# Scores and their gradient computed as rows instead of columns in a one-core attention-and-MLP training step

## The chip, the cores and the metric

The kernel runs on one core of one Trainium2 chip. The metric is device time in microseconds of one execution; lower is better. The kernel before took 407.63 us (median of three runs, 407.42 to 408.31). The core has a matrix engine (TensorE; its matmuls are listed as PE and its weight loads as PEld), a vector engine (DVE), a scalar engine (ACT), GpSimd (POOL) and SyncE (SP, which here only issues DMAs). Each engine runs its own instructions strictly in order and waits on semaphores for the others.

## The reference, cut to what matters

The reference is the forward pass and all gradients of `g * A(x) + (1 - g) * B(x)` for one token. A is decode attention over a cache of 32 heads with 4096 keys of 128 elements in bf16; B is a small MLP with the mish activation; g is a sigmoid gate. What the change touches is, for each head,

```
s  = K @ q                       # 4096 scores
p  = softmax(s / sqrt(128))
o  = p @ V                       # forward output
dp = V @ do                      # do: gradient of o
ds = p * (dp - sum(p * dp))
dq = ds @ K / sqrt(128)
dK = ds (outer) q / sqrt(128)    # 4096 x 128, written out
dV = p (outer) do                # 4096 x 128, written out
```

K and V are read once (1 MB each per head) and dK and dV are written once (1 MB each per head), so a head moves 4 MB and all of the kernel some 164 MB.

## The kernel before, in words

The program is written with every engine's order fixed by hand: instructions are issued in the order of the Python text. One loop iteration handles one head `h`; `G = 4` heads form a group, whose weights (`wq`, `wo`) and whose MLP share are mixed into the iterations by the position `hh = h % 4` and a small hand-made budget.

A K tile is stored as 128 partitions x 32 rows (`J`) x 128 elements; partition p holds keys 32p to 32p + 31. To contract over the 128 elements, the head's tile is transposed first. `tr_block` (lines 510 to 515) views eight bf16 rows as four 128x128 blocks of 4-byte words, transposes the four on TensorE into one PSUM tile (`tr`, two buffers), and copies that with ACT into the SBUF tile `KT` or `VT`. Four such blocks make a head's K or V. A row of a block is two keys of 64 words each, so after the transpose partitions 0 to 63 belong to one key and 64 to 127 to the next, and the two halves of each word (even and odd elements) are two bf16 operands, the "parities".

`cols_mm` (lines 517 to 523) then makes the scores in the layout of the K tile, 128 partitions x 32 columns. For each of 16 pairs of columns and each parity, it loads 128 transposed columns as weights and streams 32 columns of `qz`, which hold q in two of them and zeros elsewhere, so each product adds into its own two columns of the same PSUM tile: 32 weight loads and 32 matmuls. `scores` does it for S (K and q), `dP` for DP (V and do). The wide zero-padded tiles `qz` and `doz` are filled by `pair_cp` (lines 233 to 237), once a group for each.

Iteration h issues, in this order for TensorE: `v_tr(h, 0)`, `dqo_mm(h - 1)`, `v_tr(h, 1)`, the maximum over all partitions (`softmax`, line 548), `v_tr(h, 2)`, `v_tr(h, 3)`, `dP(h)`, `k_tr(h + 1, 0)`, `k_tr(h + 1, 1)`, `zd_mm` (line 566, the sums for softmax), `k_tr(h + 1, 2)`, `k_tr(h + 1, 3)`, `scores(h + 1)`, `dq_o(h)`. The last (lines 605 to 614) makes dq and o as four-row products: the stationary operand has four columns, each of four products writes its own 32-partition quarter of one PSUM tile (`od4`), and 512 elements stream through each. `od_cp` copies that tile to SBUF, and `dqo_mm` (lines 620 to 624) brings it into columns with four fp32 products with a stationary operand of 128x128 and a 0/1 matrix of two columns.

The vector engine takes, per head: the maximum's negative `negM` (line 550), `dk_out(h - 1)` (two outer products of 1.2 us each, line 581), `pj` (line 562, needs DP), `rz`, `negD`, `p`, `ds` (lines 570 to 577), `dv_out(h)` (two outer products), the row maximum `m` of the next S (line 542), and then the group's extra work. ACT takes the transposes' copies, the exponential `exps`, `dgm` (line 544, needs `m`), `od_cp` and extras. SP issues the loads of K (four buffers) and V (three) and the stores of dK and dV (four buffers).

Of the kernel before, what the change touches and what calls it, by code (L numbers as in the profile page):

```python
# [7 lines left out]
ACT = mybir.ActivationFunctionType  # L8
ALU = mybir.AluOpType
# [7 lines left out]
def kernel(  # L17
# [25 lines left out]
    P = 128  # L43
# [139 lines left out]
    dx_parts = const.tile([P, RC, NG + 3], F32, name="dx_parts")  # L183

    p4b, ds4b = [], []
    qz = const.tile([P, G, 3 * J - 2], BF16, name="qz")
    doz = const.tile([P, G, 3 * J - 2], BF16, name="doz")
    nc.gpsimd.memset(qz[:], 0.0)
    nc.gpsimd.memset(doz[:], 0.0)
    for i in range(3):  # L190
        for lst, nm in ((p4b, "p4"), (ds4b, "ds4")):
            lst.append(const.tile([P, J * 4], BF16, name=f"{nm}{i}"))
# [38 lines left out]
        return ps  # L231

    def pair_cp(z, ps):
        for par in range(2):
            nc.vector.tensor_tensor(z[:, :, J - 2 + par * J:J + par * J],
                                    ps[:, par, :].unsqueeze(2).to_broadcast([P, G, 2]),
                                    half[:].unsqueeze(1).to_broadcast([P, G, 2]), ALU.mult)

    def g_qcol(g):
        groups[g]["col"] = col_mm(groups[g]["q_row"])  # L240
# [13 lines left out]
    def g_do(g, hh):  # L254
        gp = groups[g]
        junk = small.tile([P, D], BF16, name="junk", tag="junk", bufs=1)
        nc.vector.scalar_tensor_tensor(junk[:], in0=wos[g][:, hh, :], scalar=1.0, in1=da_bc[:],  # L257
                                       op0=ALU.mult, op1=ALU.mult, accum_out=gp["do_col"][:, hh:hh + 1])
# [251 lines left out]
    def tr_block(src, dst, c):  # L510
        tp = tr_ps.tile([P, TB // 2, P], F32, name="tr", tag="tr")
        words = src[:, c * TB:(c + 1) * TB, :].rearrange("p a b -> p (a b)").bitcast(F32)
        for t in range(TB // 2):
            nc.tensor.transpose(tp[:, t, :], words[:, t * P:(t + 1) * P], ident_f[:])  # L514
        nc.scalar.copy(dst[:, c * (TB // 2):(c + 1) * (TB // 2), :], tp[:])  # L515

    def cols_mm(out, T, z):
        Tb = T[:].rearrange("p c r -> p (c r)").bitcast(BF16).rearrange("p (c r a) -> p c r a", r=P, a=2)
        for c in range(J // 2):
            for par in range(2):  # L520
                a = J - 2 - 2 * c + par * J
                nc.tensor.matmul(out, lhsT=Tb[:, c, :, par], rhs=z[:, a:a + J],  # L522
                                 start=(c == 0 and par == 0), stop=(c == J // 2 - 1 and par == 1))

    def k_tr(h, c):
        if h < H:
            if c == 0:
                KT[h] = kvT.tile([P, J // 2, P], F32, name="KT", tag="KT")
            tr_block(kts[h], KT[h], c)

    def v_tr(h, c):
        if c == 0:
            VT[h] = kvT.tile([P, J // 2, P], F32, name="VT", tag="VT")
        tr_block(vts[h], VT[h], c)

    def scores(h):
        if h >= H:
            return
        S_ps[h] = s_ps.tile([P, J], F32, name="S", tag="S")
        cols_mm(S_ps[h][:], KT.pop(h), qz[:, h % G, :])  # L540
        m32 = small.tile([P, 1], F32, name="m32", tag="m32")
        nc.vector.reduce_max(m32[:], S_ps[h][:], axis=AX.X)  # L542
        dgms[h] = small.tile([P, P], F32, name="dgm", tag="dgm", bufs=1)
        nc.scalar.activation(dgms[h][:], ident_bf[:], ACT.Copy, scale=m32[:])  # L544

# [7 lines left out]
    def exps(h, negM):  # L553
        es[h] = small.tile([P, J], BF16, name="e_bf", tag="e_bf")
        zds[h] = small.tile([P, 2], F32, name="zd", tag="zd")
        nc.scalar.activation(es[h][:], S_ps.pop(h)[:], ACT.Exp, bias=negM[:], scale=scale, accum_out=zds[h][:, 0:1])

    def dP(h):
        DP_ps[h] = s_ps.tile([P, J], F32, name="DP", tag="DP")
        cols_mm(DP_ps[h][:], VT.pop(h), doz[:, h % G, :])  # L560
        pj = small.tile([P, J], F32, name="pj", tag="pj")
        nc.vector.scalar_tensor_tensor(pj[:], in0=DP_ps[h][:], scalar=1.0, in1=es[h][:],
                                       op0=ALU.mult, op1=ALU.mult, accum_out=zds[h][:, 1:2])

    def zd_mm(h, mx):
# [2 lines left out]
    def probs(h, mx):  # L568
        rz = small.tile([P, 1], F32, name="rz", tag="rz")
        nc.vector.reciprocal(rz[:], mx[:, P:P + 1])  # L570
        negD = small.tile([P, 1], F32, name="negD", tag="negD")
        nc.vector.tensor_scalar(negD[:], mx[:, P + 1:P + 2], rz[:], -1.0, ALU.mult, ALU.mult)
        p4s[h] = p4b[h % 3][:, 0:J * 4].rearrange("p (j t) -> p j t", t=4)
        nc.vector.tensor_scalar(p4s[h], es.pop(h)[:].unsqueeze(2).to_broadcast([P, J, 4]), rz[:], None, ALU.mult)
        ds4s[h] = ds4b[h % 3][:, 0:J * 4].rearrange("p (j t) -> p j t", t=4)
        nc.vector.scalar_tensor_tensor(ds4s[h], in0=DP_ps.pop(h)[:].unsqueeze(2).to_broadcast([P, J, 4]),  # L576
                                       scalar=negD[:], in1=p4s[h], op0=ALU.add, op1=ALU.mult)
        zds.pop(h)

# [13 lines left out]
    def dv_out(h):  # L593
        out_pair(h, dVv, p4s[h], groups[h // G]["do_row"])
# [106 lines left out]
    k_tr(0, 3)  # L701
    for hh in range(G):
        g_do(0, hh)
    scores(0)
    g_dodiag(0)
    g_dobc(0)
    g_docol(0)
    g_dopair(0)
# [2 lines left out]
    for h in range(H - 1):  # L711
        g, hh = h // G, h % G
        nx, pv = g + 1 < NG, g > 0
        v_tr(h, 0)
        if hh == 0 and pv:
            g_docol(g)
        if hh == 3 and nx:
            g_qcol(g + 1)
        if h > 0:
            dqo_mm(h - 1)  # L720
        v_tr(h, 1)
        mx, negM = softmax(h)
        if h > 0:
            dqo_red(h - 1)
        if hh == 0 and pv:
            g_dopair(g)
        if h > 0:
            dk_out(h - 1)
        v_tr(h, 2)
        v_tr(h, 3)  # L730
        exps(h, negM)
        dP(h)
        k_tr(h + 1, 0)
        k_tr(h + 1, 1)
        zd_mm(h, mx)
        if hh == 0 and pv:
            f_new(g - 1)
            f_diag(g - 1)
        if hh == 1 and pv:
            f_dx(g - 1, 3)  # L740
        if hh == 2 and nx:
            g_do(g + 1, 0)
        if hh == 3 and nx:
            g_qpair(g + 1)
            g_do(g + 1, 3)
        probs(h, mx)
        if hh == 3 and nx:
            g_qpair_cp(g + 1)
        k_tr(h + 1, 2)
        k_tr(h + 1, 3)  # L750
        if hh == 0 and pv:
            f_o4(g - 1)
            f_bc(g - 1)
        if hh == 3 and nx:
            g_dodiag(g + 1)
        dv_out(h)
        scores(h + 1)
        dq_o(h)
        od_cp(h)
        load_k(h + KBUFS)  # L760
        load_v(h + VBUFS)
        if h == H - 4:
            assert dw2_next[0] == FCN
            for a, b in W2P:
                nc.sync.dma_start(dw2_v[:, a:b, :], w2_sb[:, a:b, :])
            nc.sync.dma_start(out_8[FM:F, :], w2_sb[0:FT, FR, :])
        if h == H - 2:
            assert not mq
            nc.sync.dma_start(db1_row, dh_bc[0:1, :])
            nc.sync.dma_start(dw1_v[:, 0:3, :], w1_sb[:, 0:3, :])  # L770
            nc.sync.dma_start(dw1_v[:, 3:RC, :], w1_sb[:, 3:RC, :])
        budget = 0.0
        if hh == 0:
            if nx:
                g_new(g + 1)
            if pv:
                f_o4c(g - 1)
                f_aT_pe(g - 1)
                f_dx(g - 1, 0)
                f_dx(g - 1, 1)  # L780
                f_dx(g - 1, 2)
                f_aT_add(g - 1)
                f_dwo(g - 1, 0)
                f_dwo(g - 1, 1)
            budget = 0.9
        if hh == 1:
            if pv:
                f_dx(g - 1, 4)
                for c in range(RC):
                    f_dwq(g - 1, c)  # L790
                f_dwq_st(g - 1)
                f_dwo(g - 1, 2)
                f_dwo(g - 1, 3)
                f_dwo_st(g - 1)
            budget = 2.7
        if hh == 2:
            if nx:
                g_do(g + 1, 1)
                g_do(g + 1, 2)
                g_q(g + 1)  # L800
            budget = 0.9
        if hh == 3:
            if g % 2 == 0 and g + 2 < NG:
                load_wqp(g // 2 + 1)
            if g + 2 < NG:
                load_wo(g + 2)
            if nx:
                g_dobc(g + 1)
                g_qs(g + 1)
            budget = 2.7  # L810
        if h >= 2:
            mlp_some(budget)
            dw2_some(2)
# [15 lines left out]
    v_tr(h, 2)  # L829
    v_tr(h, 3)  # L830
    exps(h, negM)
    dP(h)
    zd_mm(h, mx)
    f_bc(g, 0, 3)
# [83 lines left out]
```

## Time and profile before

| | |
|---|---|
| median of three runs | 407.63 us |
| profiled execution, its own time | 409.23 us |
| its span in the profile | 407.4 us |
| granted TensorE clock, mean over the span | 0.89 |
| matmuls of S, DP (line 522) | 34.2 and 37.0 us busy, 1024 of each |
| weight loads for them | 32.3 and 34.0 us busy |
| transposes, K and V (line 514) | 78.6 and 90.2 us busy, 512 of each |
| ACT copies of the transposes (line 515) | 69.8 and 72.6 us, 128 of each, 588 and 585 ns each |
| DVE outer products (line 581) | 150.4 us, 128 |

The profile is one execution. Its page gives each engine's busy time, the span in 40 slices, DMA queues, a chain of work followed back from the last instruction, and groups of instructions by line. Further views of the same trace give the instructions in order of time (the timeline), what an engine waited for, and busy time, clock and DMA share by windows of time. A matmul's end is modelled, so gaps between a matmul and what it releases are read between starts where possible.

### The profile page before, as it was taken

To read this page: it belongs to the slowest core of one execution; us is meant where nothing else is said; L and a number is where in the kernel's file an instruction comes from. 1 tells how busy PE (TensorE), PEld (TensorE's weight loads), DVE (VectorE), ACT (ScalarE), POOL (GpSimd) and SP (SyncE) were. 2 spreads that over 40 slices of the span, in tenths; PEclk is the share of its full clock that TensorE was granted. 3 is DMA by queue.
4 is the path that set the end of the run, shared out by engine and by line. 5 is a ranking of instruction groups with operands and counts; after the bars stand their busy time and mean duration, and the time that the engine had idled before them with its cause. 6 is when DMAs were issued, how large, how long until landed. Compare 5 with 4: busy or idle time off the path is not lost.

```text
span 407.4 us, 10856 instructions
## 1 busy us (share of the span) xinstructions
PE 332.7 (82%) x4445; PEld 271.9 (67%) x4445; DVE 306.6 (75%) x845; ACT 232.6 (57%) x479; POOL 10.0 (2%) x25
## 2 busy tenths in 40 slices
PE   2698998889898998989898898879989798989600
PEld 1487776677686977877677678758777676877500
DVE  3646774797898587998999785666899987995640
ACT  2345556666476453765567666765776553776520
POOL 3000001000000000000000003000000000000000
PEclk9989999989898597999999896787999987899755
DMA  8999999999999999999999999999999999999883
GB/s 290 427 415 422 416 414 404 403 420 421 417 421 423 422 419 421 414 426 421 424 424 425 426 418 425 416 426 422 424 408 405 426 417 425 422 386 421 359 333 133
DMA packets 28695, 164.76 MB, mean 404 GB/s; under 512 B 2916, under 2 KB 3045, under 8 KB 12262
## 3 DMA queue, kind: packets, MB, share of 16 engines
q1 hardware_dynamic: 28338, 164.05, 97.8%
q8 instruction: 35, 0.57, 0.5%
q14 instruction: 14, 0.11, 0.1%
q0 software_dynamic: 256, 0.01, 0.0%
q10 hardware_dynamic: 52, 0.01, 0.0%
HBM read 82.03 MB, written 82.03 MB: 403 GB/s over the span
## 4 chain that ended last, share of the span: by engine, by line
DVE 44%; PE 34%; ACT 10%; issue 5%; DMA 2%; DVEq 0%; ACTq 0%; SPq 0%
DVE o_sb L581 22%; PE tr L514 15%; PE dqo_ps L624 7%; DVE junk L327 3%; PE DP L522 3%; ACT od_sb L618 2%; DVE junk L257 2%; DVE ds L576 2%; DMA wq_p<-in_A_wq_dram 2%; PE q_ps L210 2%; PE od L611 2%; PE mx L548 2%; ACT KT L515 2%; ACT VT L515 2%; ACT wo_g L385 2%
## 5 line engine op out<-in xcount | busy, mean ns | idle before, releaser
L515 ACT COPY VT<-tr 128x512 f32<-128x512 f32 x128 | 72.6, 585 | 43.3 <-PE tr L514 41.4
L514 PE MATMUL tr<-ident_f,Vn 128*128 128x128 f32 x512 | 90.2, 314 | 3.4 <-ACT VT L515 1.8
L515 ACT COPY KT<-tr 128x512 f32<-128x512 f32 x128 | 69.8, 588 | 39.4 <-PE tr L514 38.7
L514 PE MATMUL tr<-ident_f,Kn 128*128 128x128 f32 x512 | 78.6, 301 | 8.7 <-DMA Kn<-in_A_k_cache_dram 5.9
L514 PEld LDWEIGHTS tr<-ident_f,Vn 128*128 128x128 f32 x512 | 69.1, 166 | 15.0 <-ACT VT L515 7.3
L581 DVE TENSOR_TENSOR o_sb<-qs_row,ds 128x2048 bf16<-128x2048 bf16 x64 | 75.2, 1217 | 0.3 <-DMA out_dram<-o_sb 0.3
L581 DVE TENSOR_TENSOR o_sb<-do_row,p 128x2048 bf16<-128x2048 bf16 x64 | 75.2, 1217 | 0.0
L514 PEld LDWEIGHTS tr<-ident_f,Kn 128*128 128x128 f32 x512 | 61.3, 154 | 13.6 <-DVE ident_f L165 5.8
L544 ACT ACTIVATE dgm<-ident_bf,m 128x128 f32<-128x128 bf16 x32 | 12.8, 401 | 57.8 <-DVE m L542 48.6
L550 DVE TENSOR_REDUCE negM<-mx 128x1 f32<-128x128 f32 x32 | 9.3, 291 | 44.8 <-PE mx L548 34.0
L624 PE MATMUL dqo_ps<-sel,od_sb 128*128 128x2 f32 x256 | 37.2, 267 | 6.8 <-ACT od_sb L618 5.1
L624 PEld LDWEIGHTS dqo_ps<-sel,od_sb 128*128 128x128 f32 x256 | 35.5, 215 | 9.7 <-ACT od_sb L618 7.3
L522 PE MATMUL DP<-doz,VT 128*128 128x32 bf16 x1024 | 37.0, 180 | 2.3
L522 PEld LDWEIGHTS <-VT 128*128 128x128 bf16 x1024 | 34.0, 100 | 6.4 <-ACT VT L515 4.3
L522 PEld LDWEIGHTS <-KT 128*128 128x128 bf16 x1024 | 32.3, 97 | 6.0 <-ACT KT L515 3.2
L522 PE MATMUL S<-qz,KT 128*128 128x32 bf16 x1024 | 34.2, 177 | 1.9
L611 PE MATMUL od<-Kn,ds 128*4 128x512 bf16 x256 | 33.3, 382 | 0.0
L611 PE MATMUL od<-Vn,p 128*4 128x512 bf16 x256 | 33.3, 382 | 0.0
L257 DVE SCALAR_TENSOR_TENSOR junk<-wo_g,da_bc 128x640 bf16<-128x640 bf16 x32 | 26.3, 820 | 0.4
L385 ACT ACTIVATE wo_g<-da_bc,o 128x640 bf16<-128x640 bf16 x32 | 24.6, 820 | 0.0
L327 DVE SCALAR_TENSOR_TENSOR junk<-wq_p,dq_bc 128x512 bf16<-128x512 bf16 x35 | 24.0, 687 | 0.5
L618 ACT COPY od_sb<-od 128x512 f32<-128x512 f32 x32 | 18.2, 568 | 1.4 <-PE od L611 1.2
(171 smaller groups left out, 337.4 us busy)
## 6 DMA issues: line engine op xcount, KB each, us to landing
out_dram<-o_sb SPq DMA_DIRECT2D x64, 1024.0 KB, 15.1
Kn<-in_A_k_cache_dram SPq DMA_DIRECT2D x32, 1024.0 KB, 17.2
Vn<-in_A_v_cache_dram SPq DMA_DIRECT2D x32, 1024.0 KB, 17.9
wq_p<-in_A_wq_dram SPq DMA_DIRECT2D x4, 1280.0 KB, 14.7
wo_g<-in_A_wo_dram SPq DMA_DIRECT2D x8, 640.0 KB, 16.9
out_dram<-wo_g SPq DMA_DIRECT2D x8, 640.0 KB, 17.5
out_dram<-wq_p SPq DMA_DIRECT2D x4, 1280.0 KB, 16.3
w_sb<-in_B_w_dram SPq DMA_DIRECT2D x1, 2160.0 KB, 23.1
```

What stands on the lines that cost most here:

```text
L257: nc.vector.scalar_tensor_tensor(junk[:], in0=wos[g][:, hh, :], scalar=1.0, in1=da_bc[:], op0=ALU.mult, op1=ALU.mult, accum_out=gp["do_col ...
L327: nc.vector.scalar_tensor_tensor(junk[:, cs], in0=wqs[g][:, c, cs], scalar=1.0, in1=gp["dq_bc"][:, cs], op0=ALU.mult, op1=ALU.mult, accum_ ...
L385: nc.scalar.activation(wos[g][:, hh, :], da_bc[:], ACT.Copy, scale=groups[g]["o4"][:, hh:hh + 1])
L514: nc.tensor.transpose(tp[:, t, :], words[:, t * P:(t + 1) * P], ident_f[:])
L515: nc.scalar.copy(dst[:, c * (TB // 2):(c + 1) * (TB // 2), :], tp[:])
L522: nc.tensor.matmul(out, lhsT=Tb[:, c, :, par], rhs=z[:, a:a + J], start=(c == 0 and par == 0), stop=(c == J // 2 - 1 and par == 1))
L544: nc.scalar.activation(dgms[h][:], ident_bf[:], ACT.Copy, scale=m32[:])
L550: nc.vector.tensor_reduce(negM[:], mx[:, 0:P], axis=AX.X, op=ALU.max, negate=True)
L581: nc.vector.tensor_tensor(dst[:, a:b, :].rearrange("p j (k t) -> p j k t", t=4), row.rearrange("p (k t) -> p k t", t=4).unsqueeze(1).to_br ...
L611: nc.tensor.matmul(od4[32 * c:32 * c + 4, :], lhsT=c4[:, 4 * jb:4 * jb + 16].rearrange("p (j t) -> p t j", t=4)[:, 0, :], rhs=N[:, jb:jb + ...
L618: nc.scalar.copy(od_sb[h][:].rearrange("p j d -> p (j d)"), od4[:])
L624: nc.tensor.matmul(od_sb[h][:], lhsT=t[:, j, :], rhs=sel[:, :, j], start=(j == 0), stop=(j == 3))
```

## The change

Four things change together.

1. `rows_mm` replaces `cols_mm`'s products. The stationary operand is now q (or do): two columns of one parity, of which the first keeps partitions 0 to 63 and the second 64 to 127 (the `half` mask; a block of 128 words holds two keys). The moving operand is the transposed K (or V), 512 elements at a step of two bf16, once for each parity and each quarter: eight matmuls. The four quarters write two rows each at partitions 0, 32, 64 and 96 of one PSUM tile `row4` (cleared once at the start).
2. ACT copies the whole `row4` (128x512 fp32) to SBUF, `row_sb`.
3. `cols_mm` is now four fp32 products that bring the rows into the old layout: the stationary operand is a 128x128 block of `row_sb`, the moving one a 0/1 matrix `sel_s` of 32 columns, which POOL makes once at the start. S and DP become the halves of one PSUM tile `sdp`.
4. `KT` and `VT` use one buffer (`tag="T"`) instead of one each. `qz` and `doz` shrink to two columns for each head and parity and are filled by one instruction instead of two.

The order changes with it: `dp_rows(h)` comes before `k_tr(h + 1, 0)` and the rest of `dP(h)` behind it; `s_rows(h + 1)` comes before `dq_o(h)` and the rest of `scores(h + 1)` behind it. In front of the loop, `g_dodiag(0)` moves ahead of `scores(0)`. In the last head nothing lies between `dp_rows` and `dP`.

```diff
-    qz = const.tile([P, G, 3 * J - 2], BF16, name="qz")
-    doz = const.tile([P, G, 3 * J - 2], BF16, name="doz")
-    nc.gpsimd.memset(qz[:], 0.0)
-    nc.gpsimd.memset(doz[:], 0.0)
+    qz = const.tile([P, 2, G, 2], BF16, name="qz")
+    doz = const.tile([P, 2, G, 2], BF16, name="doz")
+    sel_s = const.tile([P, 4, J], F32, name="sel_s")
+    nc.gpsimd.memset(sel_s[:], 0.0)
+    for i in range(2):
+        nc.gpsimd.affine_select(
+            out=sel_s[:], in_=sel_s[:], compare_op=ALU.not_equal, fill=1.0,
+            base=-3 * i, pattern=[[-8, 4], [4, J]], channel_multiplier=-1,
+        )
...
     def pair_cp(z, ps):
-        for par in range(2):
-            nc.vector.tensor_tensor(z[:, :, J - 2 + par * J:J + par * J],
...
+        nc.vector.tensor_tensor(z[:].rearrange("p a h j -> p (a h) j"),
...
-    def cols_mm(out, T, z):
-        Tb = T[:].rearrange("p c r -> p (c r)").bitcast(BF16).rearrange("p (c r a) -> p c r a", r=P, a=2)
-        for c in range(J // 2):
-            for par in range(2):
-                a = J - 2 - 2 * c + par * J
-                nc.tensor.matmul(out, lhsT=Tb[:, c, :, par], rhs=z[:, a:a + J],
-                                 start=(c == 0 and par == 0), stop=(c == J // 2 - 1 and par == 1))
+    row4 = s_ps.tile([P, 4 * P], F32, name="row4", tag="row4")
+    nc.vector.memset(row4[:], 0.0)
+    sdp = s_ps.tile([P, 2, J], F32, name="sdp", tag="sdp")
+
+    def rows_mm(T, z, hh):
+        Tb = T[:].rearrange("p c r -> p (c r)").bitcast(BF16).rearrange("p (g n a) -> p g n a", g=4, a=2)
+        for par in range(2):
+            for c in range(4):
+                nc.tensor.matmul(row4[32 * c:32 * c + 2, :], lhsT=z[:, par, hh, :], rhs=Tb[:, c, :, par],
+                                 start=(par == 0), stop=(par == 1))
+        row_sb = small.tile([P, 4, P], F32, name="row_sb", tag="row_sb", bufs=1)
+        nc.scalar.copy(row_sb[:].rearrange("p c r -> p (c r)"), row4[:])
+        return row_sb
+
+    def cols_mm(out, row_sb):
+        for c in range(4):
+            nc.tensor.matmul(out, lhsT=row_sb[:, c, :], rhs=sel_s[:, c, :], start=(c == 0), stop=(c == 3))
...
-                KT[h] = kvT.tile([P, J // 2, P], F32, name="KT", tag="KT")
+                KT[h] = kvT.tile([P, J // 2, P], F32, name="KT", tag="T")
...
-            VT[h] = kvT.tile([P, J // 2, P], F32, name="VT", tag="VT")
+            VT[h] = kvT.tile([P, J // 2, P], F32, name="VT", tag="T")
...
+    def s_rows(h):
+        if h < H:
+            rows_sb["S"] = rows_mm(KT.pop(h), qz, h % G)
...
-        S_ps[h] = s_ps.tile([P, J], F32, name="S", tag="S")
-        cols_mm(S_ps[h][:], KT.pop(h), qz[:, h % G, :])
+        S_ps[h] = sdp[:, 0, :]
+        cols_mm(S_ps[h], rows_sb.pop("S"))
...
+    def dp_rows(h):
+        rows_sb["DP"] = rows_mm(VT.pop(h), doz, h % G)
...
     def dP(h):
-        DP_ps[h] = s_ps.tile([P, J], F32, name="DP", tag="DP")
-        cols_mm(DP_ps[h][:], VT.pop(h), doz[:, h % G, :])
+        DP_ps[h] = sdp[:, 1, :]
+        cols_mm(DP_ps[h], rows_sb.pop("DP"))
...
+    s_rows(0)
+    g_dodiag(0)
     scores(0)
-    g_dodiag(0)
...
         exps(h, negM)
+        dp_rows(h)
+        k_tr(h + 1, 0)
         dP(h)
-        k_tr(h + 1, 0)
         k_tr(h + 1, 1)
...
         dv_out(h)
+        s_rows(h + 1)
+        dq_o(h)
         scores(h + 1)
-        dq_o(h)
         od_cp(h)
...
     exps(h, negM)
+    dp_rows(h)
     dP(h)
     zd_mm(h, mx)
```

More of the change, by code (lines that the diff above doesn't have):

```diff
@@ L233, in pair_cp @@
     def pair_cp(z, ps):
-        for par in range(2):
-            nc.vector.tensor_tensor(z[:, :, J - 2 + par * J:J + par * J],
-                                    ps[:, par, :].unsqueeze(2).to_broadcast([P, G, 2]),
-                                    half[:].unsqueeze(1).to_broadcast([P, G, 2]), ALU.mult)
+        nc.vector.tensor_tensor(z[:].rearrange("p a h j -> p (a h) j"),
+                                ps[:].rearrange("p a h -> p (a h)").unsqueeze(2).to_broadcast([P, 2 * G, 2]),
+                                half[:].unsqueeze(1).to_broadcast([P, 2 * G, 2]), ALU.mult)
     def g_qcol(g):
@@ L532, in v_tr @@
         if c == 0:
-            VT[h] = kvT.tile([P, J // 2, P], F32, name="VT", tag="VT")
+            VT[h] = kvT.tile([P, J // 2, P], F32, name="VT", tag="T")
         tr_block(vts[h], VT[h], c)
+    rows_sb = {}
+    def s_rows(h):
+        if h < H:
+            rows_sb["S"] = rows_mm(KT.pop(h), qz, h % G)
     def scores(h):
@@ L538, in scores @@
             return
-        S_ps[h] = s_ps.tile([P, J], F32, name="S", tag="S")
-        cols_mm(S_ps[h][:], KT.pop(h), qz[:, h % G, :])
+        S_ps[h] = sdp[:, 0, :]
+        cols_mm(S_ps[h], rows_sb.pop("S"))
         m32 = small.tile([P, 1], F32, name="m32", tag="m32")
-        nc.vector.reduce_max(m32[:], S_ps[h][:], axis=AX.X)
+        nc.vector.reduce_max(m32[:], S_ps[h], axis=AX.X)
         dgms[h] = small.tile([P, P], F32, name="dgm", tag="dgm", bufs=1)
@@ L555, in exps @@
         zds[h] = small.tile([P, 2], F32, name="zd", tag="zd")
-        nc.scalar.activation(es[h][:], S_ps.pop(h)[:], ACT.Exp, bias=negM[:], scale=scale, accum_out=zds[h][:, 0:1])
+        nc.scalar.activation(es[h][:], S_ps.pop(h), ACT.Exp, bias=negM[:], scale=scale, accum_out=zds[h][:, 0:1])
+    def dp_rows(h):
+        rows_sb["DP"] = rows_mm(VT.pop(h), doz, h % G)
     def dP(h):
-        DP_ps[h] = s_ps.tile([P, J], F32, name="DP", tag="DP")
-        cols_mm(DP_ps[h][:], VT.pop(h), doz[:, h % G, :])
+        DP_ps[h] = sdp[:, 1, :]
+        cols_mm(DP_ps[h], rows_sb.pop("DP"))
         pj = small.tile([P, J], F32, name="pj", tag="pj")
-        nc.vector.scalar_tensor_tensor(pj[:], in0=DP_ps[h][:], scalar=1.0, in1=es[h][:],
+        nc.vector.scalar_tensor_tensor(pj[:], in0=DP_ps[h], scalar=1.0, in1=es[h][:],
                                        op0=ALU.mult, op1=ALU.mult, accum_out=zds[h][:, 1:2])
@@ L575, in probs @@
         ds4s[h] = ds4b[h % 3][:, 0:J * 4].rearrange("p (j t) -> p j t", t=4)
-        nc.vector.scalar_tensor_tensor(ds4s[h], in0=DP_ps.pop(h)[:].unsqueeze(2).to_broadcast([P, J, 4]),
+        nc.vector.scalar_tensor_tensor(ds4s[h], in0=DP_ps.pop(h).unsqueeze(2).to_broadcast([P, J, 4]),
                                        scalar=negD[:], in1=p4s[h], op0=ALU.add, op1=ALU.mult)
```

## The prediction, as put on record before the changed kernel ran

> **What bounds the kernel now.** First the page: busy shares, DMA, the chain.
>
> ```profile
> PE 332.7 (82%) x4445; PEld 271.9 (67%) x4445; DVE 306.6 (75%) x845; ACT 232.6 (57%) x479; POOL 10.0 (2%) x25
> ...
> DVE 44%; PE 34%; ACT 10%; issue 5%; DMA 2%; DVEq 0%; ACTq 0%; SPq 0%
> ...
> L522 PE MATMUL DP<-doz,VT 128*128 128x32 bf16 x1024 | 37.0, 180 | 2.3
> ```
>
> No engine is full, and the chain changes between DVE, PE and ACT: the time is that of a ring of waits. The DMA share by windows is 1.01 to 1.02 from 12 to 370 us, so the DMA engines are never idle either; yet in the list of waits engines wait for DMA only some 9 us in all, nearly all at the start. So compute and transfers now run at the same pace; slower compute shows in full, faster compute would soon meet the transfers.
>
> Then the timeline of one plain head (17, DP and then S):
>
> ```profile
> 215.05 1.08 ACT L515 COPY VT<-tr 128x512 f32<-128x512 f32 x2 [0.26 <-PE tr L514]
> ...
> 215.34 1.21 PE L522 MATMUL DP<-doz,VT 128*128 128x32 bf16 x32
> ...
> 216.18 0.27 PEld L522 LDWEIGHTS <-VT 128*128 128x128 bf16 x8 [0.19 <-ACT VT L515]
> ...
> 216.86 0.18 DVE L562 SCALAR_TENSOR_TENSOR pj<-DP,e_bf 128x32 f32<-128x32 f32 x1
> ...
> 218.46 1.08 ACT L515 COPY KT<-tr 128x512 f32<-128x512 f32 x2 [0.26 <-PE tr L514]
> 218.54 2.35 DVE L581 TENSOR_TENSOR o_sb<-do_row,p 128x2048 bf16<-128x2048 bf16 x2
> ...
> 218.75 1.21 PE L522 MATMUL S<-qz,KT 128*128 128x32 bf16 x32
> ...
> 220.53 0.38 PE L611 MATMUL od<-Kn,ds 128*4 128x512 bf16 x2
> 220.54 0.38 PE L611 MATMUL od<-Vn,p 128*4 128x512 bf16 x2
> 220.81 0.18 DVE L542 TENSOR_REDUCE m<-S 128x1 f32<-128x32 f32 x1
> 220.85 0.42 PEld L514 LDWEIGHTS tr<-ident_f,Vn 128*128 128x128 f32 x4 [0.44 <-issue]
> ```
>
> See how little is left behind the transposes' last copy: 24 of 32 matmuls run ahead of it; it ends at 216.13, DP is done at 216.55. So DP is ready 0.42 us after the copy, and DVE takes it at 216.86, when its own outer products let it. S likewise: copy ends 219.54, S is done 219.96, `m` starts 220.81. In the nine heads where DVE waited for DP, `pj` starts 0.11 after the last matmul. So copy to reader is at least 0.53 us now. Gone over in the same way head by head, the room beyond it is 0.33 us on average for DP (32 heads, 10.5 us in all) and 1.05 for S (31 heads, 32.7 in all). `m` releases `dgm`, `od_cp`, `dqo_mm`, the next maximum, `negM`: in plain heads 3.01 us from `m` to `negM`, a chain without room.
>
> **The change part by part.**
>
> *Row products.* Nearest row: L611, also four 32-partition quarters with 512 columns streaming; four start together, the next four 0.21 later (219.89, 220.10, 220.32, 220.53). In `rows_mm` three of the first four run before the last copy lands; behind it the fourth quarter needs two rounds. First start 0.09 after the copy, second at 0.30. From the last L611 start to the `od_sb` copy on an idle ACT (380.71 to 381.20) 0.49 pass, so ACT starts at 0.79. That the stream steps over every second bf16 is shown by no row for a moving operand: as weights the same step costs nothing (0.097 against 0.096 for wo_g); fp32 moving operands (L548, 128 columns) also read every fourth byte and cost some 0.05 more per pass than two columns (L566). Bounds: 0.21 a round, or twice that. I take 0.21, by these rows.
>
> *Row copy.* ACT, 128x512 fp32 from PSUM: 0.57 (L618, the same shape). Done at 1.36. ACT's exponential ends 0.27 after the V copy, so it is not in the way. ACT gets 63 x 0.57 = 36 us more; at 57% busy it bears that, but the copy is on the path.
>
> *0/1 products.* Four fp32 products, stationary 128x128, 32 columns streaming. Nearest row: L624, four with the same stationary shape, eight passes, 1.05 us in head 17 (222.02). 30 more columns in each pass are 0.013 each at L548's rate, beneath the weight loads (0.12 apart). Bounds: 0.5 (one pass each) to 1.7 (L624 under the low clock, 133.80). I take 1.05. From the copy's end to the load 0.06, behind it 0.11 to the reader.
>
> Sum, DP: 1.36 + 0.06 + 1.05 + 0.11 = **2.58 us** against 0.53: +2.05. `k_tr(h+1,0)` lies in the wait for the row copy and is done by 1.3 (0.31 from the last row product to its load, as from L611 to L514 above, then 0.65).
>
> Sum, S: `dq_o` stands between. Its first round starts at 0.51, its last at 1.14; the next load 0.31 later, 1.45, so it, not the copy, sets the start; + 1.05 + 0.11 = 2.61 against 0.53: +2.08.
>
> *Ring.* From V's last copy to the next `m`, now: 162.4 us over 31 heads, 5.24 a head. New: 2.47 to the end of DP's products; to K's last copy now 2.98 from DP's end (216.55 to 219.54), later 2.80, since one of four transposes has gone ahead (0.65 + 0.35 for `zd_mm` + 1.2 + a copy of 0.6); + 2.61: **7.88**. The room is used up in this: +2.64 a head, 31 x 2.64 = 81.9. From `m` to V's last copy nothing changes: the same instructions in order, group extras of DVE, ACT and PE included, all start later with `m`.
>
> *Rest.* Last head: DP alone, +2.05. Start: S(0) goes the same way at the low clock, but `m` waited for DVE until 18.67 anyway: +1.0 (between 0.5 and 2). One buffer for K and V: each tile's first ACT copy has the row copy ahead of it in ACT's own order, which waited for the row products: 0; uncovered, 0.6 a head. One PSUM tile for S and DP: S's products stand behind `dq_o`, which needs `ds`, DP's last reader: 0. `pair_cp`: 16 instructions of 0.12 less on DVE, which now waits: 0. POOL's new masks come while POOL has 40 us without work: 0. No DMA is moved past another on SP; K and V buffers come free at the end of `dq_o`, as now.
>
> *Clock.* Head 10 shows the price:
>
> ```profile
> 129.03:144.43 15.40, 13.67 (x188) 12.41 (x184) 9.41 (x29) 7.10 (x14) 0.00 (x0) 0.67 1.01 419
> ```
>
> L624 takes 1.71 there, not 1.05, four transposes 1.09 at 135.37, not 0.65. Of the new ring's 12.5 us a plain head has some 9 on PE; 1.6 times as long is 5.4 more in 18: 0.3 us for each us at half clock. From the windows' clocks (0.98, 0.87, 0.87, 0.93 between 30 and 370) some 62 us now run at half, 17%. The ring of 440 us has a sparser PE behind `dq_o`: between 17% (+4) and a quarter (+15), I take +10; a third would be +26.
> The Trainium skill ("TensorE: Matmul & The Clock Gate", What's actually happening) says that the clock halves after a window of some 3.4 us in which the PE idles. The change's waits are each below 1 us, so by that rule the +10 would go away; the trace doesn't agree with its plain reading, since PE was busy 13.67 of 15.40 us in head 10 at a clock of 0.67.
>
> *End.* Compute ends at 391.6 now (the last outer products, 389.25 + 2.35), the span 15.8 later, since the stores are behind; after 400 the DMA share is 0.06, one engine of 16. With idle DMA time the last stores (4.1 MB from 5.4 us before the end of compute, 9.7 us at 0.42 MB/us) leave 4.3 and some 2.7 to finish: 7 (between 6 and 15.8).
>
> 391.6 + 81.9 + 2.05 + 1.0 + 10 + 7 = 493.6 of span. The profiled execution's own time is 409.23, 1.8 above its span, and 1.6 above the median of 407.63; so span + 0.2: **494 us**.
>
> **Rivals.**
> *Dearer stream:* the step of two halves the rate: two rounds, 63 x 0.42 = +26: 520. For it: no row of such a stream. Against: L548.
> *Lower clock:* a third of the ring at half clock: 510; for it head 10, against it the full clock from 30 to 89 us.
> *Cheaper 0/1 products:* 0.5 instead of 1.05, 63 x 0.52 = 33 less: 461. For it: L566's two passes take 0.28. Against: L624.
> *The change doesn't do what it says:* the quarters run one behind another; six more rounds, 63 x 1.26 = +79: 573. Against: L611 shows four at once.
> *No change:* DMA hides it. It is the fullest resource, but it delays no engine, and the queue's 15 us of landing time cover 15 us once, not 82.
> *Faster:* PE's queue sets the ring, and every wait for ACT or DVE comes only because PE was late. Now S and DP take PE 2.1 a head; later 2 x (0.42 + x), x the 0/1 products. Below x = 0.64 PE gains: with x = 0.52, 0.2 a head: 401. For it: PE 82% busy. Against: it decides only if the row copy too is hidden, and at DP the 0.33 of room is less than that copy's 0.57.
> The Trainium skill ("TensorEngine Tiling", When to Use Tiling) recommends just this swap with four column tiles where the streamed dimension is at most 32; by it the products' PE time would fall by up to four times, which is this rival.
>
> **How the numbers follow.** Forecast 0.52 (478 to 509); dearer stream or lower clock 0.22; cheaper products 0.13; quarters in turn 0.04; no change 0.03; faster 0.06. The range 453 to 532 leaves out the last three. Faster by over 0.2% 0.06, within 0.2% 0.03 (about what a measurement can tell), slower 0.91.
>
> **What would show it.** After: V's last copy to `pj` 2.6 us, K's to `m` 2.6; row copies 0.57; DVE waiting for DP in every head; row products in rounds of 0.21; L624-like 1.05 for four 0/1 products; DMA share clearly below 1; plain heads 12.5 us instead of 9.6; the end within 10 us of the last outer product. It is wrong if DP is in time for DVE, if the products take under 0.7, or if the clock is far from 0.85.

## The result, and the profile after

The changed kernel takes 484.82 us (median of 6 runs, 481.84 to 493.55), the kernel before took 407.93 us beside it (6 runs, 407.34 to 408.88): a ratio of 1.187, 95% interval 1.1832 to 1.1907. The forecast was 494 us, with a range of 453 to 532. The profiled execution is the longest of the six, and the ratio leaves it out for its lower clock: it took 493.55 us, a span of 491.7 us at a mean granted clock of 0.877, where the five others lie between 481.84 and 486.35 at 0.885 to 0.901. So its sums are about 9 us above the median, and the clock is the place to search for them. In the records of all traces here the granted clock is either 1.0 or 0.5; a mean of 0.82 over a window says that 36% of the window was at half clock.

From the page of the changed kernel, first the busy shares, then the chain of waits by engine, then three groups (count, busy us, mean ns, and the idle time before them with what ended it):

```profile
PE 421.4 (86%) x3421; PEld 297.6 (61%) x3421; DVE 309.6 (63%) x830; ACT 275.2 (56%) x543; POOL 10.1 (2%) x26
...
PE 66%; ACT 18%; DVE 7%; issue 3%; DMA 3%; DVEq 0%; ACTq 0%; SPq 0%
...
L537 PE MATMUL sdp<-sel_s,row_sb 128*128 128x32 f32 x512 | 70.6, 282 | 5.9 <-ACT row_sb L532 1.9
...
L532 ACT COPY row_sb<-row 128x512 f32<-128x512 f32 x64 | 37.5, 585 | 39.3 <-PE row L529 39.3
...
L529 PE MATMUL row<-VT,doz 128*2 128x512 bf16 x256 | 37.5, 431 | 7.8 <-ACT VT L519 7.6
```

PE issues 1,024 matmuls fewer and is busy 89 us longer: the 0/1 products (line 537) alone are 70.6 us. The row products are 37.5 (V) and 36.6 us (K), no less than the 37.0 and 34.2 of the products that they replace. The chain, which was shared by DVE (44%) and PE (34%), now lies on PE for 66% and on DVE for 7%. Before each of the 64 row copies ACT waits for the row products, 39.3 us in all: each copy starts as soon as they let it.

Head 17 in order of time, from V's last copy to the next `m`:

```profile
264.12 0.58 ACT L519 COPY VT<-tr 128x512 f32<-128x512 f32 x1 [0.27 <-PE tr L518]
...
264.76 0.61 PE L529 MATMUL row<-VT,doz 128*2 128x512 bf16 x5 [0.15 <-ACT VT L519]
...
265.30 0.66 PE L518 MATMUL tr<-ident_f,Kn 128*128 128x128 f32 x4
265.46 0.58 ACT L532 COPY row_sb<-row 128x512 f32<-128x512 f32 x1 [0.47 <-PE row L529]
...
266.10 1.08 PE L537 MATMUL sdp<-sel_s,row_sb 128*128 128x32 f32 x8
...
267.29 0.19 DVE L585 SCALAR_TENSOR_TENSOR pj<-sdp,e_bf 128x32 f32<-128x32 f32 x1 [2.24 <-PE sdp L537]
...
268.46 1.14 ACT L519 COPY KT<-tr 128x512 f32<-128x512 f32 x2 [0.19 <-PE tr L518]
...
269.65 0.64 PE L529 MATMUL row<-KT,qz 128*2 128x512 bf16 x5 [0.17 <-ACT KT L519]
...
270.39 0.58 ACT L532 COPY row_sb<-row 128x512 f32<-128x512 f32 x1 [0.79 <-PE row L529]
...
270.54 0.62 PE L634 MATMUL od<-Vn,p 128*4 128x512 bf16 x3
...
271.09 1.08 PE L537 MATMUL sdp<-sel_s,row_sb 128*128 128x32 f32 x8
272.20 0.19 DVE L562 TENSOR_REDUCE m<-sdp 128x1 f32<-128x32 f32 x1 [0.92 <-PE sdp L537]
```

Follow it link by link. V's last copy ends at 264.70, the row copy starts 0.76 later and takes 0.58, the four products start 0.06 behind it and take 1.08, and 0.11 after them DVE, idle for 2.24 us, takes `pj`: 2.59 us from copy to reader, where it was 0.73, 0.31 of that after DP was done. On the S side the copy of K ends at 269.60, the row copy at 270.97, the products start at 271.09 and `m` at 272.20: 2.60. In the heads at full clock both paths are nearly always 2.58 to 2.60. Then what DVE waited for (us in total, times, longest), before in the first line and after in the others:

```profile
DVE pj L562 <- PE DP L522: 6.8, 9, 2.2
...
DVE pj L585 <- PE sdp L537: 71.7, 32, 5.3
...
DVE m L562 <- PE sdp L537: 22.1, 25, 2.7
```

It waits for DP in all 32 heads, before in nine. Next, windows of time; behind the five engines' busy times stand the granted clock, the DMA share and GB/s:

```profile
30.00:130.00 100.00, 90.84 (x741) 62.97 (x745) 59.02 (x152) 56.93 (x115) 2.54 (x5) 0.93 0.91 353
...
245.00:350.00 105.00, 92.61 (x715) 65.33 (x714) 64.02 (x167) 65.28 (x126) 3.23 (x2) 0.82 0.88 331
...
480.00:491.70 11.70, 0.27 (x1) 0.09 (x1) 2.79 (x5) 0.54 (x2) 0.56 (x1) 0.50 0.74 294
```

The DMA share is 0.88 to 0.93 in the loop, no longer 1.01. The last number of the next two lines is the median time from a store's issue to its landing, before and after:

```profile
out_dram<-o_sb SPq DMA_DIRECT2D x64, 1024.0 KB, 15.1
...
out_dram<-o_sb SPq DMA_DIRECT2D x64, 1024.0 KB, 5.3
```

Loads of K land after 8.6 us (17.2 before) and of V after 10.7 (17.9): the queue has drained, and the transfers run at the pace of compute.

Adding up the stretches between fixed events in both profiled executions gives the whole difference:

| stretch | before, us | after, us | difference | forecast |
|---|---|---|---|---|
| start to the first `m` | 18.67 | 20.63 | +2.0 | +1.0 |
| V's last copy to the next `m`, 31 heads | 162.4 | 237.1 | +74.7 | +81.9 and most of the clock's +10 |
| `m` to V's last copy, 31 heads | 190.9 | 199.6 | +8.7 | 0, and the rest of the clock's +10 |
| last `m` to the end of the last outer product | 19.6 | 25.6 | +6.0 | +2.05 |
| from there to the end of the span | 15.8 | 8.8 | -7.0 | -8.8 |
| sum (491.7 - 407.4) | | | +84.3 (rounding) | +86.2 |

### The profile page after: what moved, and what is told of

It is laid out like the page before. It is cut to its first block, busy times and chain, and to the rows that moved or that the text cites. A ratio compares the mean times of both kernels' runs of the same rounds, so it can differ in the third digit from the quotient of the medians.

```text
span 491.7 us, 8862 instructions
## 1 busy us (share of the span) xinstructions
PE 421.4 (86%) x3421; PEld 297.6 (61%) x3421; DVE 309.6 (63%) x830; ACT 275.2 (56%) x543; POOL 10.1 (2%) x26
## 4 chain that ended last, share of the span: by engine, by line
PE 66%; ACT 18%; DVE 7%; issue 3%; DMA 3%; DVEq 0%; ACTq 0%; SPq 0%
PE tr L518 22%; PE sdp L537 14%; PE row L529 10%; PE dqo_ps L647 7%; PE od L634 6%; ACT VT L519 5%; ACT row_sb L532 4%; ACT KT L519 4%; PE mx L568 2%; DMA wq_p<-in_A_wq_dram 2%; ACT od_sb L641 2%; ACT dgm L564 2%; PE mx L589 1%; DVE m L562 1%; DVE o_sb L604 1%
## 5 line engine op out<-in xcount | busy, mean ns | idle before, releaser
L518 PE MATMUL tr<-ident_f,Vn 128*128 128x128 f32 x512 | 103.7, 353 | 1.8 <-ACT VT L519 1.6
L519 ACT COPY KT<-tr 128x512 f32<-128x512 f32 x128 | 73.8, 586 | 44.3 <-PE tr L518 44.2
L518 PEld LDWEIGHTS tr<-ident_f,Vn 128*128 128x128 f32 x512 | 84.0, 191 | 6.9 <-ACT VT L519 4.2
L537 PEld LDWEIGHTS sdp<-sel_s,row_sb 128*128 128x128 f32 x512 | 63.6, 195 | 28.2 <-ACT row_sb L532 25.8
L537 PE MATMUL sdp<-sel_s,row_sb 128*128 128x32 f32 x512 | 70.6, 282 | 5.9 <-ACT row_sb L532 1.9
L532 ACT COPY row_sb<-row 128x512 f32<-128x512 f32 x64 | 37.5, 585 | 39.3 <-PE row L529 39.3
L585 DVE SCALAR_TENSOR_TENSOR pj<-sdp,e_bf 128x32 f32<-128x32 f32 x32 | 6.1, 192 | 71.7 <-PE sdp L537 71.7
L529 PE MATMUL row<-VT,doz 128*2 128x512 bf16 x256 | 37.5, 431 | 7.8 <-ACT VT L519 7.6
L634 PE MATMUL od<-Vn,p 128*4 128x512 bf16 x256 | 41.5, 392 | 0.0
L529 PE MATMUL row<-KT,qz 128*2 128x512 bf16 x256 | 36.6, 401 | 5.1 <-ACT KT L519 3.0
L634 PE MATMUL od<-Kn,ds 128*4 128x512 bf16 x256 | 34.6, 393 | 0.0
## 6 DMA issues: line engine op xcount, KB each, us to landing
Vn<-in_A_v_cache_dram SPq DMA_DIRECT2D x32, 1024.0 KB, 10.7
```

Source lines behind the costliest of these rows:

```text
L529: nc.tensor.matmul(row4[32 * c:32 * c + 2, :], lhsT=z[:, par, hh, :], rhs=Tb[:, c, :, par], start=(par == 0), stop=(par == 1))
L532: nc.scalar.copy(row_sb[:].rearrange("p c r -> p (c r)"), row4[:])
L537: nc.tensor.matmul(out, lhsT=row_sb[:, c, :], rhs=sel_s[:, c, :], start=(c == 0), stop=(c == 3))
L634: nc.tensor.matmul(od4[32 * c:32 * c + 4, :], lhsT=c4[:, 4 * jb:4 * jb + 16].rearrange("p (j t) -> p t j", t=4)[:, 0, :], rhs=N[:, jb:jb + ...
```

## The experiments

Times are medians, ratios are to the kernel before on the same chip. All stand on the changed kernel, except the three that fill the kernel before.

**One buffer or two.** `KT` and `VT` get their own buffers again; the space for it comes from the small tiles behind `p` and `ds` (three to two) and from `pj`.

```diff
-                KT[h] = kvT.tile([P, J // 2, P], F32, name="KT", tag="T")
+                KT[h] = kvT.tile([P, J // 2, P], F32, name="KT", tag="KT")
...
-            VT[h] = kvT.tile([P, J // 2, P], F32, name="VT", tag="T")
+            VT[h] = kvT.tile([P, J // 2, P], F32, name="VT", tag="VT")
```

> The changed kernel with KT and VT in a buffer each again (room for it comes from two instead of three p4/ds4 tiles and one pj tile). Theory A (the path from the last transposed copy to the reader of S and DP has grown by some 2.05 us at each of 63 places, and the room of 0.33 and 1.05 us is used up): nothing waits for the one buffer, so 484 to 486 us as the changed kernel. Rival C (the one buffer holds up the first copy of the next transposed tile, up to 0.6 us a head at two places): 484.8 - 63 x 0.6 = 447 us if all of it, above 475 if it is small.

Measured: 484.28 us, ratio 1.1858 (1.1828 to 1.1889); the change has 1.187 (1.1832 to 1.1907). The shared buffer costs nothing that can be measured. Its profiled execution (span 480.6, clock 0.891) also serves as a second trace of the change, nearer to the median: its last outer product ends at 471.8, and from 30 to 445 us it has 79 us at half clock where the change's trace has 88.

**S alone by rows.** DP goes back to 32 products with V's transpose standing; so that both forms fit, S shares a PSUM tile with the maxima, and DP has its own.

```diff
-        DP_ps[h] = sdp[:, 1, :]
-        cols_mm(DP_ps[h], rows_sb.pop("DP"))
+        DP_ps[h] = dpt[:]
+        cols32(DP_ps[h], VT.pop(h), doz[:, h % G, :])
...
-        dp_rows(h)
```

> Only S goes through rows; DP is made by 32 products in columns as before, in a PSUM tile of its own, and S shares a PSUM tile with mx. Theory A: S costs 2.58 - 0.53 - 1.05 = 1.0 us in each of 31 heads, so 407.9 + 31 to 35 = 439 to 443 us. Rival B (TensorE's own work sets the time; its busy time rose by 89 us, the same for S as for DP): half of the 77 us, 446 us; what tells A from B is that S only comes out clearly below DP only.

**DP alone by rows.** The mirror image: S by 32 products again, before `dq_o` as in the kernel before.

```diff
-        S_ps[h] = sdp[:, 0, :]
-        cols_mm(S_ps[h], rows_sb.pop("S"))
+        S_ps[h] = smx[:, 0:J]
+        cols32(S_ps[h], KT.pop(h), qz[:, h % G, :])
...
-        s_rows(h + 1)
-        dq_o(h)
+        dq_o(h)
```

> Only DP goes through rows; S is made by 32 products in columns as before. Theory A: DP costs 2.05 - 0.33 = 1.72 us in each of 32 heads and its delay is passed on to the next m: 407.9 + 55 = 463 us, some 20 us above S only. Rival B: 446 us, the same as S only.

Measured: S alone 432.88 us, 1.061 (1.0555 to 1.0665); DP alone 456.61 us, 1.1189 (1.1172 to 1.1206). The waits of DVE, S alone first:

```profile
DVE m L578 <- PE smx L545: 28.7, 32, 1.2
...
DVE pj L601 <- PE dpt L552: 6.8, 11, 2.2
```

and DP alone:

```profile
DVE pj L601 <- PE dpt L545: 69.8, 31, 5.3
```

Each half brings its own wait and leaves the other as it was. At full clock the path from copy to reader is nearly the same in both profiles (2.58 for S, 2.52 for DP), yet DP costs more: by the end of the last outer product +54.1 us against +34.1. Nearly all of it lies between V's last copy and the next `m`: that stretch grows by 52.4 us with DP alone and by 31.6 with S alone. Both forms together give +80.2 in the second trace above and +91.3 in the profiled execution; the halves add up to 88.2. So the price of a half is the grown path less the room beyond it (1.05 us a head at S, 0.33 at DP). A fuller PE is not the cause: its busy time rises by 40 us with S alone and by 45 with DP alone (373.0 and 377.9 against 332.7), and the costs are not nearly as equal. S alone was profiled in its longest execution, 3.4 us above its median and with more time at half clock (108 us from 30 to 445, DP alone 79), so the clock doesn't explain the difference either. Both expectations were 6 to 10 us high at the total mainly because they left out that the end shrinks, by 7 us, once compute is slow enough for the stores to be out.

**The 0/1 products in bf16.** `row_sb` and `sel_s` in bf16, so S and DP are rounded to bf16 on the way; nothing else changes.

```diff
-    sel_s = const.tile([P, 4, J], F32, name="sel_s")
+    sel_s = const.tile([P, 4, J], BF16, name="sel_s")
...
-        row_sb = small.tile([P, 4, P], F32, name="row_sb", tag="row_sb", bufs=1)
+        row_sb = small.tile([P, 4, P], BF16, name="row_sb", tag="row_sb", bufs=1)
```

> The changed kernel, with row_sb and the 0/1 matrix in bf16, so that the four products load bf16 weights once each (S and DP are rounded to bf16 on the way, which the reference does not do). Theory A: the products take some 0.35 us instead of 1.08, the path gets shorter by that at 63 places (S by less, since the products stand behind dq_o): 484.8 - 63 x 0.7 = 441 us, between 436 and 450. If the clock alone were the cause of the loss, TensorE's less work would lower it further and the time would stay above 470.

Measured: 430.76 us, 1.0553 (1.0523 to 1.0583). From its timeline:

```profile
37.00 0.58 ACT L532 CAST row_sb<-row 128x512 bf16<-128x512 f32 x1 [0.48 <-PE row L529]
...
37.64 0.27 PE L537 MATMUL sdp<-sel_s,row_sb 128*128 128x32 bf16 x4
...
38.01 0.19 DVE L585 SCALAR_TENSOR_TENSOR pj<-sdp,e_bf 128x32 f32<-128x32 f32 x1 [0.83 <-PE sdp L537]
```

Four products take 0.27 us in place of 1.08, the copy still 0.58, and DP's path is 1.77 us in place of 2.58 in heads at full clock. S's falls nearly as far, but not in the last head of each group, where `m` still comes 2.39 us behind the copy (2.22 in the kernel before). The time falls by 54 us. Against the second trace, 43.7 of that lie between V's last copy and the next `m` (235.9 to 192.2), which is the expected 44: nearly all of the saving comes back. Another 5.6 lie between `m` and V's last copy (192.8 to 187.2), where nothing was changed; up to the last outer product this run has 21 us less at half clock (75 against 96). What is left, 22 us above the kernel before, is copy and handovers: the path is still 1.77 us where at least 0.53 was, which makes the stretch 29.8 us longer, and the end is 7 us shorter.

**No cover.** The order of the change is undone, so that nothing lies between row products and 0/1 products.

```diff
-        dp_rows(h)
-        k_tr(h + 1, 0)
+        k_tr(h + 1, 0)
+        dp_rows(h)
         dP(h)
...
-        s_rows(h + 1)
-        dq_o(h)
+        dq_o(h)
+        s_rows(h + 1)
         scores(h + 1)
```

> The changed kernel with the order undone: the 0/1 products directly behind the row products (k_tr(h+1, 0) and dq_o(h) behind them), so that TensorE stands still during the row copy. Its work is the same. Theory A (path): DP is ready as before, but K's transposes end some 0.6 us later; S is ready at the same time, but dq_o, od_cp and dqo_mm some 0.6 us later: + 31 x 1.15 = +36, 520 us (510 to 530). Rival B (TensorE's own work sets the time): its work is unchanged, 485 us.

Measured: 1.2424 (1.239 to 1.2459) from the two executions at the higher clock, 505.12 (0.936) and 508.26 us (0.923); two more took 524.72 (0.887) and 529.29 us (0.877). Its timeline, profiled at 0.923:

```profile
198.47 0.58 ACT L532 COPY row_sb<-row 128x512 f32<-128x512 f32 x1 [0.47 <-PE row L529]
...
199.11 1.08 PE L537 MATMUL sdp<-sel_s,row_sb 128*128 128x32 f32 x8 [0.73 <-ACT row_sb L532]
...
200.02 1.07 PE L518 MATMUL tr<-ident_f,Kn 128*128 128x128 f32 x8
200.29 0.19 DVE L585 SCALAR_TENSOR_TENSOR pj<-sdp,e_bf 128x32 f32<-128x32 f32 x1 [1.65 <-PE sdp L537]
```

PE now stands idle for 0.73 us while ACT copies, then has eight transposes of K to do, not four. Copy to `pj` stays 2.58, but `pj` to K's last copy grows from 2.32 to 2.86, and `m` to V's last copy grows too: at full clock from 5.40 to 6.47 in the last head of each group of four, from 5.32 to 5.81 in the first, and as much in the third (4.84, read in the run with fillers in half of the heads, to 5.33). 0.54 x 31 - 0.07 x 31 (K's copy to `m` falls to 2.51) + 1.07 x 7 + 0.49 x 16 is 30 us. Some 22 are found at a higher clock than the change had and some 40 at a clock like its own (0.887), so the sum lies between the two. So the order of the change does hide PE's other work behind the row copy, as the forecast's sum assumed. The rival, that PE's load alone sets the ring and the order is no matter (485 us), falls.

**Filling PE's waits.** Three matmuls whose result nobody needs, 512 columns each, stand before `dqo_mm`, where PE waits for ACT's copy of `od` in some heads (nine, by the trace of the change):

```profile
PE dqo_ps L647 <- ACT od_sb L641: 6.5, 9, 0.7
```

The edit:

```diff
+    def fill(n):
+        for i in range(n):
+            nc.tensor.matmul(row4[:], lhsT=ident_bf[:], rhs=da_bc[:, 0:4 * P], start=True, stop=True)
...
+            fill(3)
             dqo_mm(h - 1)
```

> The changed kernel with three products more (128x128 stationary, 512 columns of bf16, results not used) in front of each dqo_mm, where TensorE waits 0.7 us for od_sb: 20 us more work for TensorE, none of it on the path if it fits. Rival B: +20, 505 us. Theory A without the clock: 485 to 489. Theory A with the clock as in the prediction (TensorE too sparse behind dq_o, some 77 to 92 us of the loop at half clock, 0.3 us lost for each): the half-clock time falls, 465 to 478 us.

Measured: 489.18 us, 1.1994 (1.1971 to 1.2018): not 465 to 478, and no gain at all. The fillers leave values in rows of `row4` that `sel_s` also takes up, so S and DP carry them along; that changes neither the instructions nor their order.

```profile
46.95 0.81 PE L541 MATMUL row<-da_bc,ident_bf 128*128 128x512 bf16 x3
...
47.22 0.56 ACT L645 COPY od_sb<-od 128x512 f32<-128x512 f32 x1
...
47.84 1.05 PE L651 MATMUL dqo_ps<-sel,od_sb 128*128 128x2 f32 x8
```

Two things came out of it. The stretch at half clock up to the last outer product did shrink, from 96 us (the two-buffer run) to 58, by the windows' clocks (twice the missing share of each window's length). But in most heads PE has other work at that place and no wait to fill. In the first and last head of a group `dqo_mm` starts 0.66 later (1.90 to 2.56 behind `m` in the last), `negM` 0.56 later, and `m` to V's last copy is 5.96 instead of 5.40 in the last. The price is a little above the gain, 489.18 against 484.82; the run says nothing on the clock's price alone.

The same in the kernel before, with two matmuls (and in a second kernel four more ahead of V's third transposes in the third head of a group), into DP's bank:

```diff
+    def fill(h, n):
+        for i in range(n):
+            nc.tensor.matmul(DP_ps[h][:], lhsT=ident_bf[:], rhs=da_bc[:, 0:4 * P], start=True, stop=True)
...
+            fill(h, 2)
             dqo_mm(h - 1)
```

> The kernel before with two such unused products in front of each dqo_mm (into the DP tile's bank). If the clock costs what the prediction says, some of the 62 us of the loop at half clock go: 400 to 406 us, no lower than some 398, where the transfers end; if the fillers only delay dqo_mm, 408 to 412.

> As the last one, and four more unused products in front of the third V transposes in every third head of a group, where TensorE waits for ACT's extra work. Clock: below the last one, 398 to 404; if it only delays: 2 to 6 us above the last one.

Measured: 410.23 us, 1.0061 (1.0048 to 1.0074), and 409.9 us, 1.0065 (1.0044 to 1.0087), at clocks of 0.91 to 0.935 where the kernel before beside them had 0.894 to 0.918. Again the clock rises and the time does not fall: in the first of the two, `m` to V's last copy grows by 5.8 us over 31 heads and V's last copy to the next `m` shrinks by 3.9.

**Filling in half of the heads.** The fillers stand in the second and third head of each group alone, and their stationary operand is zero, so that S and DP stay as they are. In the trace of the change PE waits before `dqo_mm` in nine of these 16 heads, for 0.72 to 0.96 us; in the seven others the fillers are added work (`dqo_mm` starts 2.14 us behind `m` in place of 1.49 in second heads).

```diff
+            if hh in (1, 2):
+                fill(3)
             dqo_mm(h - 1)
```

> The changed kernel with the three unused products only in every second and third iteration of a group, where the trace of the fill in all iterations shows dqo_mm undelayed (in the others it was 0.56 us late); the stationary operand is zero, so that S and DP stay those of the changed kernel. Theory with the clock (0.3 us for each us at half clock in the loop): about half of the fall in half-clock time of the fill in all iterations (from 96 to 58 us up to the last outer product) without its price: 470 to 479 us. If the clock costs nothing on the path: 484 to 486.

Measured: 476.92 us, 1.1648 (1.1605 to 1.1691), below the change's interval: 8 us less, as expected. Two windows of its profile (its shortest execution, span 469.5, clock 0.944), then the second of them from the two-buffer run and from the run without cover:

```profile
30.00:130.00 100.00, 92.17 (x791) 61.37 (x795) 63.58 (x170) 58.89 (x120) 2.54 (x5) 1.00 0.93 366
...
245.00:350.00 105.00, 92.50 (x774) 63.01 (x780) 68.95 (x174) 69.20 (x134) 3.23 (x2) 0.93 0.90 346
...
245.00:350.00 105.00, 93.60 (x748) 65.23 (x748) 65.80 (x168) 68.71 (x134) 3.24 (x2) 0.88 0.91 345
...
245.00:350.00 105.00, 86.45 (x753) 58.21 (x754) 68.04 (x178) 62.29 (x123) 3.24 (x2) 0.97 0.89 339
```

The granted clock is 1.00 and 0.93 where the change had 0.93 and 0.82. From 30 to 445 us some 24 us are at half clock, 79 in the two-buffer run and 88 in the change. So the fillers raise the clock, and the time falls with it: the low clock costs time here.

Why they raise it is not shown. PE's busy share doesn't explain it: from 30 to 445 us PE is busy for 375.9 us with the fillers and for 375.7 in the two-buffer run. Nor do its short waits alone: without cover PE waits more and is busy for only 350.7 us, and yet in two of that version's four executions, the profiled one among them (57 us at half clock), the clock is above that of every execution of the change. Whether it is the place of the fillers or their kind (512 columns of bf16, where most of PE's work here is fp32 or has few columns) was not tried.

The kernel before, with two fillers in the same heads:

> The kernel before with the two unused products only in the same iterations, where they delay nothing. With the clock alone 403 to 406 us; if the transfers, whose engines are never idle until 370 us, hold the end, 406 to 408, no difference from the kernel before; slower than 409 only if the fillers still delay.

Measured: 408.3 us, 1.0002 (0.9991 to 1.0013), at 0.908 to 0.929. There a higher clock is worth nothing: its last outer product ends at 391.8 and the transfers 15.8 later, as without fillers. Two waits for DMA in its profile have grown, from 0.3 and 0.8 us before:

```profile
DVE o_sb L587 <- DMA out_dram<-o_sb: 3.5, 2, 2.4
...
PE tr L514 <- DMA Vn<-in_A_v_cache_dram: 3.2, 4, 1.0
```

So some of what compute gains in that kernel it spends in waiting for transfers, which fits a DMA share of 1.01; no run tried it with fewer bytes.

No version tried is faster than the kernel before.

## Why the prediction was right

*What bounds.* This was right. The kernel before is a ring of waits with no engine full, and DMA runs at the same pace: the slower compute showed in full up to the last outer product, and the DMA share fell below 1. The forecast that faster compute would soon meet the transfers fits the last run above.

*Row products.* This was right. The last round starts 0.28 us after the copy (0.30 forecast), and the row copy 0.48 behind that (0.49). The rounds are 0.21 to 0.22 apart, as those of line 634 are, so the step of two in the stream costs nothing, and the "dearer stream" and the "quarters one behind another" did not happen.

*Row copy.* It takes 0.58 (0.57 forecast) and is on the path.

*0/1 products.* They take 1.08 (1.05 forecast), with 0.06 before and 0.11 behind. DP's path is 2.58 as forecast, S's 2.58 to 2.60 (2.61); `dq_o` does set the start of S's products, 0.11 to 0.12 behind the copy. That both rooms are used up is shown by the halves: +54 and +34 with nearly equal paths.

*Ring.* One term of the sum was mis-sized: from `pj` to K's last copy it is 2.32 a head, where 2.69 was forecast (2.80 from the end of DP's products, less 0.11). `zd_mm` starts 0.25 after `pj`, and the last eight transposes and their copy follow more closely than the sum of their rows. 0.37 x 31 is 11.5 us. At full clock the grown ring is 2.58 + 2.32 + 2.58 = 7.48 a head, so its term is 2.24 x 31 = 69.5, not 81.9.

*Start and last head.* They grew by 2.0 and 6.0 us, where 1.0 and 2.05 were forecast. In the last head the clock is low, 0.70 from 445 to 480 us; in the two-buffer run the two grew by 1.0 and 3.9.

*Clock.* The amount was right: 21% of 30 to 445 us is at half clock (17% to a quarter forecast), 26 us more than the 62 of the kernel before (30 to 370). The price was on the low side. Within one program it is seen from run to run, between the shortest and the longest execution: with the order undone, 24 us for some 65 us more at half clock, 0.4 for each; in the change itself, 11.7 us for 26, 0.45; 0.3 was forecast. The fillers give 0.2 (11 us by the last outer product for 55), but they take PE's time too. These are differences between executions, and no run varied the clock alone. In the profiled execution 14 us are put down to the clock (74.7 - 69.5 in the one stretch, 8.7 in the other) where 10 was forecast; in the two-buffer run, with 17 us more at half clock than before, it is 6 (73.5 - 69.5 and 1.9). Which price holds for a single head stays open.

So the forecast meets the profiled execution (493.55 us) because its errors offset each other, and that is luck: the ring -12, against clock +4, start +1, last head +4 and end +2. The median, at a higher clock, lies 9 us below it.

The page "TensorE: Matmul & The Clock Gate" of the Trainium skill (What's actually happening) ties the halving to an idle window of about 3.4 us. The trace of the change doesn't agree with the plain reading: between 30 and 445 us PE never stands idle for longer than 2.67 us (from 333.6 to 336.3), and yet the clock goes to half there 20 times. What brings it down in this kernel stays open.

*End.* It is 8.8 us where 7 was forecast; the stores are out early.

*Rivals.* "Cheaper 0/1 products" is what bf16 makes true, at 0.27, with 431 us and not less than before: the condition that the "faster" rival named, x below 0.64, is met there and PE is still not the bound, because the copy remains on the path. That settles the "faster" rival. The page "TensorEngine Tiling" of the Trainium skill (When to Use Tiling), which recommends the swap, is not borne out here: the row products keep PE busy for 74.1 us (at a mean clock of 0.877) where the products before took 71.2 (0.890), and the way back into columns comes on top. A "lower clock" of a third of the ring at half is above the 21% seen. "No change" fell with the measured time, and the DMA share with it.

## What to carry to other kernels

Price a swap of operands by the latency from the last input to the first reader, with the handovers and the copy that bring the result back into its layout, and take off only the room that the trace shows at that reader. Here 24 of 32 cheap matmuls lay ahead of the last copy, and of what replaced them only three of eight row products did: two nearly equal paths of 2.52 and 2.58 us cost 54 and 34 us, about what the 0.33 and 1.05 us of room a head say. A saving on such a path came back almost in full here (bf16), where the transfers had room; whether it would do so below the time of the kernel before was not tried.

## What the hardware did that was not expected

- Four fp32 products with a 128x128 stationary operand and 32 columns take 1.08 us, the same in bf16 0.27: a quarter, although the profile counts only twice as many matmuls for fp32 (eight, not four).
- A bf16 stream that steps over every second element runs at the pace of L634's, 0.21 to 0.22 us from one round of four quarters of 512 columns to the next.
- The granted clock went to half without any PE wait above 2.67 us in the loop, for 3.4 us or a multiple (6.8, 13.7) each time. In the profiled executions three unneeded matmuls in each of 16 heads took 55 of 79 us at half clock away at the same busy share of PE; why is open.
- The version without cover took 505 to 529 us in four executions, the longer the lower the clock that it was granted, where the kernel before varies by 1.7.
